# Local and global attention ahead of a feed-forward layer: block transposes on VectorE with an exchange through HBM, from the fifth pair of heads on

## The chip, the cores and the metric

The kernel runs on one core of a Trainium2 chip, as one launch. The metric is the device time of an execution in microseconds; several executions are timed and their median is compared. One more execution was taken with the hardware profiler, and all rows of a profile come from it. The engines are PE (TensorE matmul; PEld is its weight load), DVE (VectorE), ACT (ScalarE), POOL (GpSimd) and SP (SyncE, which issues all DMAs here).

## What is computed

A batch of 8 with 8 heads of 64: 512 local tokens attend to a window of 32 tokens to either side and to 32 global tokens; the 32 global tokens attend to everything. The attention output, 4608 rows of 512, goes through a feed-forward layer with a leaky activation whose slope is per feature. All is float32.

```python
s_ll = np.where(np.abs(pos[:, None] - pos[None, :]) <= 32, scale * q_l @ k_l.T, -1e9)
out_l = sm(concat([scale * q_l @ k_g.T, s_ll])) @ concat([v_g, v_l])
out_g = sm(scale * q_g @ concat([k_g, k_l]).T) @ concat([v_g, v_l])
x = concat([out_g, out_l]).transpose(0, 2, 1, 3).reshape(4608, 512)
h = x @ w_in
return (np.maximum(h, 0) + alpha * np.minimum(h, 0)) @ w_out
```

## The kernel before

**Pairs.** Two heads make a pair P (0 to 31; `NPAIR` = 4 pairs make a batch). Local attention of a pair has four parts. `local_scores` does 32 small matmuls (one for each of 16 windows of 32 queries and each head h, 64 rows deep, 128 keys wide) into two PSUM banks `s_ps`. `local_softmax` works on them: DVE scales, masks and takes a minimum (`p`, `mn`), ACT takes eight exponentials with sums. `local_transposes` lets PE transpose the probabilities `p` (eight 128x128 transposes into `pt`), and ACT and DVE copy one bank each to SBUF. `local_values` multiplies with the values `vw` into `o_ps`, and DVE scales by `rz` into `xq`. `local_outputs` lets PE transpose `xq` (four transposes, `xt`), and ACT copies them into `x_raw`, where the batch's four pairs lie side by side.

**Feed-forward.** 9 groups (8 batches of 512 local columns, then all 256 global columns) times 16 slices of the hidden width make 144 steps t. In step t `f1(t)` does 12 matmuls into a bank `h_ps`; ACT and DVE make `g` of it, ACT rounds `g` to `gh`, and POOL takes the rest `gl`. `f2` of the step two earlier does 8 matmuls with `gh` (part 0) and 4 with `gl` (part 1) into four output banks. These 24 matmuls are 512 columns wide, or 256 in the last group. Inputs and weights are split into a rounded part and a rest, hence three matmuls for each product. The 16 weight tiles `ws` arrive as words that DVE and ACT decode into `wt` during the first steps.

**Global attention.** 16 blocks k of two pairs: `global_scores` (`g_ps`), `global_transposes` (`gt`), `global_values` (`go`), `global_outputs` (again in the bank of `go`, into `x_glb`).

**Order.** Pairs 0 to 3 run ahead of step 0, with PE transposes and their own branch. All others are placed by hand: `plan(t, where, fn, P)` puts a part into step t ahead of f1 ("pre"), between f1 and f2 ("mid"), or between the two parts of f2 ("post"). Each pair has four steps: scores in "pre" of the first, transposes in "pre" of the third, values in its "post", outputs in "mid" of the fourth. A scheduler then sets the order on every engine; matmuls stay in program order. Each engine works its list in order, and SP issues its DMAs in order, waiting where a source or a buffer isn't ready.

**PSUM.** `h_ps` has two banks (tag "h"); s_ps, pt, o_ps, xt and all global parts of the later pairs share two others (tag "s"); four hold the outputs. `qk` and `vw` of the later pairs have one buffer each.

Of the kernel before, what the change touches and what calls it, by code (L numbers as in the profile page):

```python
# [8 lines left out]
F32 = mybir.dt.float32  # L9
# [8 lines left out]
NB, NH, SL, SG, D = 8, 8, 512, 32, 64  # L18
# [12 lines left out]
TC = dict(schedule_with_timeline_sim=True)  # L31
HP = 50
HPU = 4
PAD = (0, 0)
LAG = 2
NDEC = 2
NLOAD = 3
# [12 lines left out]
    return 32 * (3 * (i // 2) + i % 2)  # L50


@with_exitstack
def longformer_ffn(ctx: ExitStack, tc: tile.TileContext, qk, vs, gn, vg, w, alpha, out):
    nc = tc.nc
# [3 lines left out]
    work = ctx.enter_context(tc.tile_pool(name="work", bufs=1))  # L59
    psum = ctx.enter_context(tc.tile_pool(name="psum", bufs=1, space=PS))  # L60
    wpool = ctx.enter_context(tc.tile_pool(name="wpool", bufs=NWB))

    alpha_sb = const.tile([128, NF + PAD[0]], F32, name="alpha_sb")[:, 0:NF]
    mask = const.tile([128, 4, 128], F32, name="mask")
# [10 lines left out]
    def matmul(*a, **k):  # L75
        return tc.keep_in_program_order(nc.tensor.matmul(*a, **k))  # L76
# [4 lines left out]
    def stage(name, dtype=F32):  # L81
        return work.tile([128, 512], dtype, tag="st", name=name, bufs=NST)
# [10 lines left out]
    def bank(tag, name):  # L93
        return psum.tile([128, 512], F32, tag=tag, name=name, bufs=2 if tag in "hs" else 1)
# [29 lines left out]
    def wide(name, dtype=F32):  # L124
        return work.tile([128, 1024], dtype, tag="dec", name=name, bufs=3)
# [49 lines left out]
    def local_scores(P):  # L175
        t = qks.pop(P)
        tags = ("o0", "o1", "o2", "o3") if P < NPAIR else ("s", "s", "s", "s")
        for h in range(2):
            ps_of[P, h] = bank(tags[2 * (P % 2) + h], "s_ps")
            if P < NPAIR:  # L180
                matmul(ps_of[P, h], ident_bf, mask_bf, start=True, stop=False)
        for i in range(NWIN):
            for h in range(2):
                hs = slice(64 * h, 64 * h + 64)
                k0 = SL + window(i)
                r0, c0 = 32 * (i % 4), 128 * (i // 4)
                matmul(ps_of[P, h][r0 : r0 + 32, c0 : c0 + 128], t[hs, 32 * i : 32 * i + 32], t[hs, k0 : k0 + 128], start=P >= NPAIR, stop=P >= NPAIR or i >= NWIN - 4)

    def local_softmax(P):
        z = small("z", 8)  # L190
# [19 lines left out]
    def local_transposes(P):  # L210
        for h in range(2):
# [4 lines left out]
            pt_of[P, h] = stage("pt")  # L216
            copy("ad"[h], pt_of[P, h], ps)

    xs = {}

    def split(src, n):
        xh, xl = stage("xh", F32R), stage("xl", F32R)
        nc.scalar.copy(xh[:, 0:n], src)
        nc.vector.tensor_tensor(xl[:, 0:n], src, xh[:, 0:n].bitcast(F32), op=ALU.subtract)  # L224
        return xh, xl

    def local_values(P):
        o = bank("h" if P < NPAIR else "s", "o_ps")
        v = vws.pop(P)
        for i4 in range(4):  # L230
            for h in range(2):
                for k in range(4):
                    i = 4 * i4 + k
                    c = 128 * i4 + 64 * h
                    matmul(o[32 * k : 32 * k + 32, c : c + 64], pt_of[P, h][:, 32 * i : 32 * i + 32], v[:, i % 2, i // 2, 64 * h : 64 * h + 64], start=True, stop=True)
        z, rz = z_of.pop(P), small("rz", 8)
        nc.scalar.activation(rz, z, AF.Copy, bias=1e-9)
        nc.vector.reciprocal(rz, rz)
        xq = stage("xq")
        nc.vector.tensor_tensor(xq.rearrange("q (g d) -> q g d", g=8), o.rearrange("q (g d) -> q g d", g=8), sub_ap(rz, 0, 128, 0, ((1, 8), (0, 64))), op=ALU.mult)  # L240
        xq_of[P] = xq

    def local_outputs(P):
        b, p = divmod(P, NPAIR)
        xq = xq_of.pop(P)
        ps = bank("h" if P < NPAIR else "s", "xt")
        for i in range(4):
            transpose(ps[:, 128 * i : 128 * i + 128], xq[:, 128 * i : 128 * i + 128], ident)
        if P < NPAIR:
            xs[0, p] = split(ps, SL)  # L250
        else:
            nc.scalar.copy(x_raw[:, p], ps)  # L252

    gns, vgs, sgs, gz, gout = {}, {}, {}, {}, {}

    def load_global(k, what):
        for P in (2 * k, 2 * k + 1):
            if what == "gn":
                gns[P] = wide("gn")[:, 0:576]
                nc.sync.dma_start(gns[P], gn[P])  # L260
            else:
                vgs[P] = wide("vg")[:, 0:640].rearrange("k (y d) -> k y d", y=5)
                nc.sync.dma_start(vgs[P], vg[P])

    def global_scores(k):
        ss = [bank("s", "g_ps") for h in range(2)]
        for h in range(2):
            nc.vector.memset(ss[h][64:128, 256:288], -3.0e38)
        for r, c0, n in ((0, 32, 288), (1, 320, 256)):
            for e in range(2):  # L270
                t = gns[2 * k + e]
                for h in range(2):
                    hs, q0 = slice(64 * h, 64 * h + 64), 64 * r + 32 * e
                    matmul(ss[h][q0 : q0 + 32, 0:n], t[hs, 0:32], t[hs, c0 : c0 + n], start=True, stop=True)
        for e in range(2):
            del gns[2 * k + e]
        m, z = small("gm", 4), small("gz", 4)
        sg_sb = sgs[k] = wide("sg")[:, 0:576].rearrange("q (h n) -> q h n", h=2)
        for h in range(2):
            nc.vector.tensor_reduce(m[:, h : h + 1], ss[h][:, 0:288], axis=AX.X, op=ALU.max)  # L280
        nc.vector.tensor_scalar(m[:, 2:4], m[:, 0:2], -0.125, None, op0=ALU.mult)
        nc.vector.tensor_copy(m[0:64, 0:2], m[64:128, 2:4])
        nc.vector.tensor_tensor(m[0:64, 2:4], m[0:64, 2:4], m[0:64, 0:2], op=ALU.min)
        nc.vector.tensor_copy(m[64:128, 2:4], m[0:64, 2:4])
        for h in range(2):
            nc.scalar.activation(sg_sb[:, h], ss[h][:, 0:288], AF.Exp, bias=m[:, 2 + h : 3 + h], scale=0.125, accum_out=z[:, h : h + 1])
        nc.vector.tensor_copy(z[0:64, 2:4], z[64:128, 0:2])
        nc.vector.scalar_tensor_tensor(z[0:64, 2:4], z[0:64, 2:4], 1e-9, z[0:64, 0:2], op0=ALU.add, op1=ALU.add)
        nc.vector.reciprocal(z[0:64, 2:4], z[0:64, 2:4])
        nc.vector.tensor_copy(z[64:128, 2:4], z[0:64, 2:4])  # L290
        gz[k] = z
# [11 lines left out]
                nc.vector.transpose(sgt_sb[0:32, 4, h, 32 * e : 32 * e + 32], sg_sb[32 * e : 32 * e + 32, h, 256:288])  # L303

    def global_values(k):
        ps = bank("s", "go")
        for y in range(5):
            for h in range(2):
                for e in range(2):
                    q0 = 64 * h + 32 * e  # L310
                    matmul(ps[q0 : q0 + 32, 0:64], sgt_sb[:, y, h, 32 * e : 32 * e + 32], vgs[2 * k + e][:, y, 64 * h : 64 * h + 64], start=(y == 0), stop=(y == 4))
        for e in range(2):
            del vgs[2 * k + e]
        z = gz.pop(k)
        for h in range(2):
            hs = slice(64 * h, 64 * h + 64)
            nc.scalar.activation(og_sb[hs, hs], ps[hs, 0:64], AF.Copy, scale=z[hs, 2 + h : 3 + h])
        gout[k] = ps

    def global_outputs(k):  # L320
        ps = gout.pop(k)
        b, p = divmod(2 * k, NPAIR)
        matmul(ps[:, 64:128], og_sb, pick, start=True, stop=True)
        nc.scalar.copy(x_glb[:, p : p + 2, SG * b : SG * b + SG], ps[:, 64:128].rearrange("d (e q) -> d e q", e=2))
# [54 lines left out]
    def plan(t, where, fn, P):  # L379
        at.setdefault((t, where), []).append((fn, P))  # L380

    for P in range(NPAIR, NPR):
        base = 4 * (P - NPAIR)
        plan(base, "pre", local_scores, P)
        plan(base, "pre", local_softmax, P)
        plan(base + 2, "pre", local_transposes, P)
        plan(base + 2, "post", local_values, P)
        plan(base + 3, "mid", local_outputs, P)
        if P > NPAIR:
            plan(base - 4, "mid", load_qk, P)  # L390
            plan(base - 1, "post", load_v, P)
    begin = [16] + [20 + 8 * i for i in range(12)] + [112, 116, 120, 128]
    for k in range(NPR // 2):
        t = begin[k]
        late = begin[k + 1] - t < 8 or t == 120
        plan(t - 1, "mid", lambda k: load_global(k, "gn"), k)
        plan(t, "post", global_scores, k)
        plan(t + 1, "mid", lambda k: load_global(k, "vg"), k)
        when = ((2, "post"), (3, "mid"), (3, "post")) if late else ((3, "pre"), (6, "post"), (7, "mid"))
        for (dt, where), fn in zip(when, (global_transposes, global_values, global_outputs)):  # L400
            plan(t + dt, where, fn, k)

    def attention(t, where):
        for fn, P in at.pop((t, where), ()):
# [27 lines left out]
    load_next(NLOAD)  # L432
    load_qk(NPAIR)
    load_v(NPAIR)

    def scores(P):
        local_scores(P)
        local_softmax(P)

    keep_warm(6)  # L440
    scores(0)
# [94 lines left out]
```

## Time and profile before

| What | Value |
|---|---|
| median of 3 runs (lowest, highest) | 985.55 us (984.82, 986.91) |
| profiled execution, its time | 984.07 us |
| its span (first to last instruction) | 982.3 us |
| granted TensorE clock, mean | 0.981 |
| DMA packets and bytes | 88110, 102.55 MB |
| time of the packets, share of 16 engines | 31.0% |

A row of the timeline has the start, the length to the end of the last instruction in it, engine, line, operation, out<-in, shape and count. Matmuls overlap, so the pitch between starts and not the length tells what one costs. Small float32 matmuls show as two instructions each. A row of groups has the busy time, the mean length of one in ns, and the idle time of the engine ahead of it with what ended it. DMA rows end with KB and the median time from issue to landing.

### The profile page before, as it was taken

Reading aid. Unit: us, or ns where it says so; the run is one execution under the profiler, and the core shown is the slowest. Engines: PE = TensorE matmul, PEld = TensorE weight load, DVE = VectorE, ACT = ScalarE, POOL = GpSimd, SP = SyncE. Lnnn points to the kernel's source line nnn. Section 1 sums busy time; section 2 is a strip of 40 time slices with the busy share of each in tenths; the row PEclk is TensorE's granted clock in tenths of the full one; section 3 lists DMA queues with packets and bytes.
Section 4 is the critical chain, followed back from the end, with each engine's and each line's share of the span. In section 5 each row is a group of like instructions: output and inputs, shape, how many; then the busy total and the mean of one; then the engine's idle time right before and its main releaser. Section 6 shows DMA issues by size and latency. Waiting matters only on the chain.

```text
span 982.3 us, 21069 instructions
## 1 busy us (share of the span) xinstructions
PE 942.5 (96%) x8962; PEld 752.0 (77%) x8962; DVE 388.3 (40%) x765; ACT 421.2 (43%) x1139; POOL 183.3 (19%) x161
## 2 busy tenths in 40 slices
PE   5588899999999999999999999999999999999997
PEld 3466688778777887878787878878777777778797
DVE  4899952532342323332343224232343234222211
ACT  4776743543444334433453333443454333322232
POOL 1002221212111222122121112212212112222221
PEclk8788999999999999999999999999999999999999
DMA  9935432332324323322334223332233221210010
GB/s 317 379 144 206 139 96 72 116 106 84 111 85 135 102 67 100 127 67 73 110 103 135 84 84 108 102 110 69 73 126 111 84 83 27 93 51 28 0 44 22
DMA packets 88110, 102.55 MB, mean 104 GB/s; under 512 B 3536, under 2 KB 69584, under 8 KB 85968
## 3 DMA queue, kind: packets, MB, share of 16 engines
q1 hardware_dynamic: 88016, 101.21, 31.0%
q8 instruction: 70, 1.15, 0.5%
q14 instruction: 24, 0.20, 0.1%
HBM read 92.28 MB, written 8.91 MB: 103 GB/s over the span
## 4 chain that ended last, share of the span: by engine, by line
PE 87%; DVE 7%; SPq 2%; issue 1%; ACT 1%; DMA 1%; DVEq 0%; ACTq 0%
PE o L76 38%; PE h_ps L76 37%; PE o_ps L76 3%; PE s_ps L76 3%; PE pt L79 2%; SPq L171 1%; DVE wt L140 1%; PE go L76 1%; PE xt L79 1%; DVE wt L142 1%; DVE wt L137 1%; DVE wt L149 1%; PE g_ps L76 1%; DMA ws<-in_w_dram 1%; PE gt L79 1%
## 5 line engine op out<-in xcount | busy, mean ns | idle before, releaser
L76 PE MATMUL h_ps<-xh,wt 128*128 128x512 f32 (+1 forms) x1152 | 351.6, 388 | 0.0
L349 POOL TENSOR_TENSOR gl<-g,gh 128x512 fp32r<-128x512 f32 (+1 forms) x144 | 178.8, 1242 | 791.1 <-ACT gh L348 714.9
L76 PE MATMUL o<-gh,wt 128*128 128x512 f32 (+1 forms) x1152 | 279.7, 385 | 0.0
L76 PEld LDWEIGHTS h_ps<-xh,wt 128*128 128x128 f32 x1152 | 208.3, 189 | 45.6 <-issue 4.5
L76 PEld LDWEIGHTS o<-gh,wt 128*128 128x128 f32 x1152 | 206.6, 188 | 43.0
L346 DVE SCALAR_TENSOR_TENSOR g<-g,beta_sb,h_ps 128x512 f32<-128x512 f32 (+1 forms) x144 | 103.1, 716 | 319.4 <-ACT g L345 319.0
L76 PE MATMUL h_ps<-xl,wt 128*128 128x512 f32 (+1 forms) x576 | 220.6, 383 | 0.8 <-DVE xl L224 0.8
L345 ACT ACTIVATE g<-h_ps 128x512 f32<-128x512 f32 (+1 forms) x144 | 82.0, 569 | 223.6 <-PE h_ps L76 206.4
L76 PE MATMUL o<-gl,wt 128*128 128x512 f32 (+1 forms) x576 | 156.1, 393 | 0.0
L206 ACT ACTIVATE p<-p,mn 128x128 f32<-128x128 f32 x224 | 86.8, 390 | 107.4 <-DVE mn L203 107.4
L348 ACT CAST gh<-g 128x512 fp32r<-128x512 f32 (+1 forms) x144 | 85.9, 596 | 109.2 <-DVE g L346 109.1
L76 PEld LDWEIGHTS h_ps<-xl,wt 128*128 128x128 f32 x576 | 108.6, 189 | 24.0 <-DVE xl L224 1.2
L76 PEld LDWEIGHTS o<-gl,wt 128*128 128x128 f32 x576 | 101.5, 189 | 27.6 <-issue 7.2
L202 DVE SCALAR_TENSOR_TENSOR p<-s_ps,mask 128x512 f32<-128x512 f32 x56 | 36.0, 683 | 60.5 <-PE s_ps L76 60.5
L76 PEld LDWEIGHTS o_ps<-vw,pt 128*32 128x32 f32 x2048 | 31.5, 113 | 16.9 <-issue 10.4
L91 DVE COPY pt<-pt 128x512 f32<-128x512 f32 x32 | 22.1, 689 | 55.5 <-PE pt L79 55.5
L206 ACT ACTIVATION_READ_ACCUMULATOR p<-p,mn 128x1 f32 x224 | 42.0, 187 | 0.0
L76 PE MATMUL o_ps<-vw,pt 128*32 128x64 f32 x2048 | 37.1, 226 | 4.9 <-DVE pt L91 3.9
L79 PE MATMUL pt<-ident,p 128*128 128x128 f32 x256 | 37.2, 288 | 4.6 <-ACT p L206 4.5
L76 PEld LDWEIGHTS s_ps<-qk 64*32 64x32 f32 x2048 | 30.2, 110 | 13.6 <-issue 12.7
L79 PEld LDWEIGHTS pt<-ident,p 128*128 128x128 f32 x256 | 32.0, 147 | 10.7 <-issue 4.8
L76 PE MATMUL s_ps<-qk 64*32 64x128 f32 x2048 | 39.4, 285 | 0.7 <-ACT x_raw L252 0.7
(76 smaller groups left out, 565.5 us busy)
## 6 DMA issues: line engine op xcount, KB each, us to landing
vw<-in_vs_dram SPq DMA_DIRECT2D x64, 512.0 KB, 5.2
qk<-in_qk_dram SPq DMA_DIRECT2D x32, 672.0 KB, 4.0
ws<-in_w_dram SPq DMA_DIRECT2D x16, 1024.0 KB, 9.2
vg<-in_vg_dram SPq DMA_DIRECT2D x32, 320.0 KB, 3.1
gn<-in_gn_dram SPq DMA_DIRECT2D x32, 288.0 KB, 4.7
out_dram<-ost SPq DMA_DIRECT2D x32, 256.0 KB, 2.3
out_dram<-ost SPq DMA_DIRECT2D x4, 128.0 KB, 2.4
alpha_sb<-in_alpha_dram SPq DMA_DIRECT2D x1, 8.0 KB, 1.7
```

What stands on the lines that cost most here:

```text
L76: return tc.keep_in_program_order(nc.tensor.matmul(*a, **k))
L79: return tc.keep_in_program_order(nc.tensor.transpose(*a))
L91: nc.vector.tensor_copy(dst, src)
L137: nc.vector.tensor_scalar(t, t, CLAMP_LO, CLAMP_HI, op0=ALU.max, op1=ALU.min)
L140: nc.vector.scalar_tensor_tensor(tu, high, 0xC0000000, tu, op0=ALU.bitwise_and, op1=ALU.bitwise_or)
L142: nc.vector.tensor_tensor(ti, ti, r, op=ALU.add)
L202: nc.vector.scalar_tensor_tensor(p, s, -0.125, mask.rearrange("q i n -> q (i n)"), op0=ALU.mult, op1=ALU.add)
L206: nc.scalar.activation(p3[:, i], src[:, i], AF.Exp, bias=mn[:, i : i + 1], scale=scale, accum_out=z[:, k : k + 1])
L345: nc.scalar.activation(g[:, 0:n], h[:, 0:n], AF.Relu, scale=-1.0)
L346: nc.vector.scalar_tensor_tensor(g[:, 0:n], g[:, 0:n], beta_sb[:, f : f + 1], h[:, 0:n], op0=ALU.mult, op1=ALU.add)
L348: nc.scalar.copy(gh[:, 0:n], g[:, 0:n])
L349: nc.gpsimd.tensor_tensor(gl[:, 0:n], g[:, 0:n], gh[:, 0:n].bitcast(F32), op=ALU.subtract)
```

## The change

Four parts, all for pairs from the fifth on (P >= 4).

**Transposes.** `exchange` has DVE transpose the sixteen 32x32 blocks of a 128x512 tile in one instruction, with the blocks in another order, writes the tile to HBM in one DMA (128 rows of 2 KB), and reads it back in four (32 partitions each, 512 bytes a row), which puts the blocks on their partitions. It takes the place of the PE transposes and their copies, once for each head's probabilities (`pb`, into `pt`) and once for the output (`xb`, straight into `x_raw`). `place` numbers the windows so that blocks and windows agree.

**Order.** A pair's scores come in "post" of step turn[P], its values in "post" of turn[P+1], directly ahead of the next pair's scores. Turns are 0, 3, 7, 10, 13, then every four steps from 17.

**Global parts.** o_ps and go move from the "s" banks to the two "h" banks. The 16 blocks are spread evenly over steps 17 to 124; values of one block stand directly ahead of scores of the next; outputs get a place and a bank (`gx`) of their own. `gn` and `sg` live in one weight slot.

**Addresses.** `PAD` makes two tiles larger, which moves what is allocated behind them. Of the staging tiles (the moving operands of f1 and f2) the address in a partition was 256 bytes past a multiple of 512 and is a multiple of 512; of the weight tiles it was 128 past one and is a multiple.

```diff
-PAD = (0, 0)
+PAD = (64, 32)
+def place(P, c, wd):
+    return 4 * c + wd if P < NPAIR else 4 * wd + c
...
+    def exchange(src, put, name):
+        blk = stage(name)
+        nc.vector.transpose(blk.rearrange("k (b c n) -> k c b n", b=4, c=4), src.rearrange("q (c b n) -> q c b n", c=4, b=4))
+        spread = dram.tile([128, 4, 128], F32, tag=name, name=name, bufs=2)
+        nc.sync.dma_start(spread, blk.rearrange("k (b n) -> k b n", b=4))
+        for b in range(4):
+            nc.sync.dma_start(put[32 * b : 32 * b + 32].rearrange("k (w n) -> k w n", w=4), spread[:, b].rearrange("(w k) n -> k w n", w=4))
+
+    def local_exchange(P):
+        for h in range(2):
+            pt_of[P, h] = stage("pt")
+            exchange(pr_of.pop((P, h)), pt_of[P, h], "pb")
...
     def local_values(P):
-        o = bank("h" if P < NPAIR else "s", "o_ps")
+        o = bank("h", "o_ps")
...
-        xq_of[P] = xq
+        if P < NPAIR:
+            xq_of[P] = xq
+        else:
+            exchange(xq, x_raw[:, P % NPAIR], "xb")
...
     def global_values(k):
-        ps = bank("s", "go")
+        ps = bank("h", "go")
...
     def global_outputs(k):
-        ps = gout.pop(k)
+        ps = bank("s", "gx")
...
+    turn = {4: 0, 5: 3, 6: 7, 7: 10, 8: 13}
     for P in range(NPAIR, NPR):
-        base = 4 * (P - NPAIR)
-        plan(base, "pre", local_scores, P)
-        plan(base, "pre", local_softmax, P)
-        plan(base + 2, "pre", local_transposes, P)
-        plan(base + 2, "post", local_values, P)
-        plan(base + 3, "mid", local_outputs, P)
+        u = turn.setdefault(P + 1, 4 * (P - NPAIR) + 1)
+        plan(u, "post", values, P)
+        if P == NPAIR:
+            plan(turn[P], "post", scores, P)
+        if P + 1 < NPR:
+            plan(u, "post", scores, P + 1)
+            plan(turn[P] + 1, "post", load_qk, P + 1)
+            plan(u + 1, "post", load_v, P + 1)
...
+        plan(u, "mid", global_scores, k)
+        plan(v - 2, "mid", global_transposes, k)
+        at.setdefault((v, "mid"), []).insert(0, (global_values, k))
+        plan(v + 1, "mid", global_outputs, k)
```

On PE, in the middle of the program, between the two parts of an f2 (`o_` and a number are the four output banks; x32 counts matmuls), before:

```order
L76 MATMUL o_4318<-gh,wt 128x512 x2
L76 MATMUL o_ps<-vw,pt 32x64 x32
L76 MATMUL go<-vg,sgt_sb 32x64 x20
L76 MATMUL o_4315<-gl,wt 128x512
L76 MATMUL o_4316<-gl,wt 128x512
```

On PE at the same place, now:

```order
L81 MATMUL o_4552<-gh,wt 128x512 x2
L81 MATMUL o_ps<-vw,pt 32x64 x32
L81 MATMUL s_ps<-qk 32x128 x32
L81 MATMUL o_4549<-gl,wt 128x512
L81 MATMUL o_4550<-gl,wt 128x512
```

The scores of the next pair stand behind the values, and the global values have gone elsewhere.

On DVE during the decoding of the weights (`wt` is a weight tile being decoded, ISA one of its operations), before, up to the eighth `g`:

```order
L346 SCALAR_TENSOR_TENSOR g<-g,beta_sb,h_ps 128x512
L142 ISA wt<-wt,wr 128x2048
L137 TENSOR_SCALAR wt<-wt 128x1024
L240 TENSOR_TENSOR xq<-o_ps,rz 128x512
L139 TENSOR_SCALAR wt<-wt 128x1024
L149 TENSOR_TENSOR wt<-wt 128x2x512
L140 SCALAR_TENSOR_TENSOR wt<-ws,wt 128x1024
L346 SCALAR_TENSOR_TENSOR g<-g,beta_sb,h_ps 128x512
```

On DVE with as many weights decoded, now, up to the fifth `g`:

```order
L145 SCALAR_TENSOR_TENSOR wt<-ws,wt 128x1024
L228 STREAM_TRANSPOSE pb<-p 128x4x4x32
L147 ISA wt<-wt,wr 128x2048
L142 TENSOR_SCALAR wt<-wt 128x1024
L144 TENSOR_SCALAR wt<-wt 128x1024
L154 TENSOR_TENSOR wt<-wt 128x2x512
L145 SCALAR_TENSOR_TENSOR wt<-ws,wt 128x1024
L368 SCALAR_TENSOR_TENSOR g<-g,beta_sb,h_ps 128x512
```

The transpose of pair 5 stands where values of pair 5 stood, and three fewer steps have been through.

On SP in the steady part, before (loads of the next pairs and global blocks):

```order
L171 DMA vw<-in_vs_dram 128x8x128 x2
L260 DMA gn<-in_gn_dram 128x576
L160 DMA qk<-in_qk_dram 128x1344
L263 DMA vg<-in_vg_dram 128x640 x2
L171 DMA vw<-in_vs_dram 128x8x128 x2
```

On SP in the steady part, now:

```order
L176 DMA vw<-in_vs_dram 128x8x128 x2
L230 DMA xb<-xb 128x512
L165 DMA qk<-in_qk_dram 128x1344
L232 DMA x_raw<-xb 32x4x128 x4
L230 DMA pb<-pb 128x512
L286 DMA vg<-in_vg_dram 128x640 x2
L281 DMA gn<-in_gn_dram 128x576
L232 DMA pt<-pb 32x4x128 x4
L230 DMA pb<-pb 128x512
L281 DMA gn<-in_gn_dram 128x576
L232 DMA pt<-pb 32x4x128 x4
```

The 15 transfers of an exchange stand among the loads, each write ahead of the four reads that wait for its landing.

More of the change, by code (lines that the diff above doesn't have):

```diff
@@ L61, in longformer_ffn @@
     wpool = ctx.enter_context(tc.tile_pool(name="wpool", bufs=NWB))
+    dram = ctx.enter_context(tc.tile_pool(name="dram", bufs=1, space=bass.MemoryType.DRAM))
     alpha_sb = const.tile([128, NF + PAD[0]], F32, name="alpha_sb")[:, 0:NF]
@@ L181, in local_scores @@
                 matmul(ps_of[P, h], ident_bf, mask_bf, start=True, stop=False)
-        for i in range(NWIN):
+        for j in range(NWIN):
+            c, wd = divmod(j, 4)
+            i = place(P, c, wd)
             for h in range(2):
@@ L185, in local_scores @@
                 k0 = SL + window(i)
-                r0, c0 = 32 * (i % 4), 128 * (i // 4)
-                matmul(ps_of[P, h][r0 : r0 + 32, c0 : c0 + 128], t[hs, 32 * i : 32 * i + 32], t[hs, k0 : k0 + 128], start=P >= NPAIR, stop=P >= NPAIR or i >= NWIN - 4)
+                r0, c0 = 32 * wd, 128 * c
+                matmul(ps_of[P, h][r0 : r0 + 32, c0 : c0 + 128], t[hs, 32 * i : 32 * i + 32], t[hs, k0 : k0 + 128], start=P >= NPAIR, stop=P >= NPAIR or c == 3)
     def local_softmax(P):
@@ L232, in local_values @@
                 for k in range(4):
-                    i = 4 * i4 + k
+                    i = place(P, i4, k)
                     c = 128 * i4 + 64 * h
@@ L240, in local_values, with load_gn, load_vg @@
         nc.vector.tensor_tensor(xq.rearrange("q (g d) -> q g d", g=8), o.rearrange("q (g d) -> q g d", g=8), sub_ap(rz, 0, 128, 0, ((1, 8), (0, 64))), op=ALU.mult)
-        xq_of[P] = xq
+        if P < NPAIR:
+            xq_of[P] = xq
+        else:
+            exchange(xq, x_raw[:, P % NPAIR], "xb")
     def local_outputs(P):
-        b, p = divmod(P, NPAIR)
         xq = xq_of.pop(P)
-        ps = bank("h" if P < NPAIR else "s", "xt")
+        ps = bank("h", "xt")
         for i in range(4):
             transpose(ps[:, 128 * i : 128 * i + 128], xq[:, 128 * i : 128 * i + 128], ident)
[L249 to L256, printed above, removed]
-        for P in (2 * k, 2 * k + 1):
[L258 to L263, printed above, removed]
+        xs[0, P] = split(ps, SL)
+    gns, vgs, sgs, gz = {}, {}, {}, {}
+    big = []
+    def load_gn(k):
+        if not big:
+            big.append(wpool.tile([128, 2048], F32, tag="w", name="gn"))
+        for e in range(2):
+            gns[2 * k + e] = big[0][:, 576 * e : 576 * e + 576]
+            nc.sync.dma_start(gns[2 * k + e], gn[2 * k + e])
+    def load_vg(k):
+        for P in (2 * k, 2 * k + 1):
+            vgs[P] = wide("vg")[:, 0:640].rearrange("k (y d) -> k y d", y=5)
+            nc.sync.dma_start(vgs[P], vg[P])
     def global_scores(k):
@@ L277, in global_scores @@
         m, z = small("gm", 4), small("gz", 4)
-        sg_sb = sgs[k] = wide("sg")[:, 0:576].rearrange("q (h n) -> q h n", h=2)
+        sg_sb = sgs[k] = big[0][:, 1152:1728].rearrange("q (h n) -> q h n", h=2)
         for h in range(2):
@@ L317, in global_values @@
             nc.scalar.activation(og_sb[hs, hs], ps[hs, 0:64], AF.Copy, scale=z[hs, 2 + h : 3 + h])
-        gout[k] = ps
     def global_outputs(k):
-        ps = gout.pop(k)
+        ps = bank("s", "gx")
         b, p = divmod(2 * k, NPAIR)
@@ L380, in plan, with scores, values @@
         at.setdefault((t, where), []).append((fn, P))
-    for P in range(NPAIR, NPR):
-        base = 4 * (P - NPAIR)
-        plan(base, "pre", local_scores, P)
-        plan(base, "pre", local_softmax, P)
-        plan(base + 2, "pre", local_transposes, P)
-        plan(base + 2, "post", local_values, P)
-        plan(base + 3, "mid", local_outputs, P)
[L389 to L392, printed above, removed]
-    for k in range(NPR // 2):
[L394 to L401, printed above, removed]
+    def scores(P):
+        local_scores(P)
+        local_softmax(P)
+        if P >= NPAIR:
+            local_exchange(P)
+    def values(P):
+        local_values(P)
+    turn = {4: 0, 5: 3, 6: 7, 7: 10, 8: 13}
+    for P in range(NPAIR, NPR):
+        u = turn.setdefault(P + 1, 4 * (P - NPAIR) + 1)
[6 more added lines that the diff above has]
+            plan(u + 1, "post", load_v, P + 1)
+    step = []
+    for j in range(NPR // 2 + 1):
+        u = 17 + 107 * j // 16
+        step.append(u + (u % 4 == 1))
+    for k in range(NPR // 2):
+        u, v = step[k], step[k + 1]
+        plan(u - 2, "mid", load_gn, k)
+        plan(u, "mid", global_scores, k)
+        plan(u + 1, "mid", load_vg, k)
+        plan(v - 2, "mid", global_transposes, k)
+        at.setdefault((v, "mid"), []).insert(0, (global_values, k))
+        plan(v + 1, "mid", global_outputs, k)
     def attention(t, where):
@@ L434, in longformer_ffn @@
     load_v(NPAIR)
-    def scores(P):
-        local_scores(P)
-        local_softmax(P)
     keep_warm(6)
```

## The prediction

> **What bounds the kernel now.** I read the page first, then busy time by stage, then the chain of waits where the stages meet.
>
> ```profile
> span 982.3 us, 21069 instructions
> PE 942.5 (96%) x8962; PEld 752.0 (77%) x8962; DVE 388.3 (40%) x765; ACT 421.2 (43%) x1139; POOL 183.3 (19%) x161
> PE 87%; DVE 7%; SPq 2%; issue 1%; ACT 1%; DMA 1%; DVEq 0%; ACTq 0%
> ```
>
> ```profile
> 64.00:122.46 58.46, 50.89 (x449) 39.69 (x449) 57.57 (x64) 41.70 (x78) 11.54 (x8) 0.93 0.57 204
> 122.46:925.00 802.54, 802.54 (x7450) 636.95 (x7450) 274.30 (x610) 323.93 (x925) 154.84 (x121) 1.00 0.28 89
> ```
>
> ```profile
> 117.92 0.66 PE xt L79 x4
> 118.58 2.79 PE o L76 x12
> 121.37 1.09 PE s_ps L76 x64
> 122.46 2.98 PE h_ps L76 x12
> ```
>
> The columns of the stage rows are stretch, length, PE, PEld, DVE, ACT, POOL, clock, DMA share, GB/s. Up to 122.46 DVE is the bound (57.57 of 58.46 us): it decodes the weights. From 122.46, where f1(8) starts behind the scores of pair 6, PE is never idle (802.54 of 802.54). So work taken from PE after that is worth its full price, and before that nothing.
>
> **The change part by part.** The timeline of PE (start, length) prices its blocks:
>
> ```profile
> 301.78 1.10 PE L76 MATMUL o_ps<-vw,pt 128*32 128x64 f32 x64
> 302.70 0.74 PE L76 MATMUL go<-vg,sgt_sb 128*32 128x64 f32 x40
> ...
> 307.19 0.60 PE L79 MATMUL xt<-ident,xq 128*128 128x128 f32 x4
> 307.63 0.33 PE L76 MATMUL go<-pick,og_sb 128*128 128x64 f32 x2
> 307.77 2.11 PE L76 MATMUL o<-gh,wt 128*128 128x512 f32 x8
> 309.72 1.08 PE L76 MATMUL o<-gl,wt 128*128 128x512 f32 x4
> 310.73 1.16 PE L76 MATMUL s_ps<-qk 64*32 64x128 f32 x64
> 311.81 0.73 PE L76 MATMUL h_ps<-xh,wt 128*128 128x512 f32 x2
> ...
> 312.61 0.64 PE L76 MATMUL h_ps<-xh,wt 128*128 128x512 f32 x2
> ...
> 321.11 2.03 PE L76 MATMUL o<-gh,wt 128*128 128x512 f32 x8
> 322.97 1.09 PE L76 MATMUL o<-gl,wt 128*128 128x512 f32 x4
> 323.90 1.03 PE L79 MATMUL pt<-ident,p 128*128 128x128 f32 x8
> ...
> 325.47 0.63 PE L76 MATMUL h_ps<-xh,wt 128*128 128x512 f32 x2
> ...
> 327.56 2.03 PE L76 MATMUL o<-gh,wt 128*128 128x512 f32 x8
> 329.53 1.10 PE L76 MATMUL o_ps<-vw,pt 128*32 128x64 f32 x64
> 330.56 1.20 PE L76 MATMUL o<-gl,wt 128*128 128x512 f32 x4
> 331.60 0.60 PE L79 MATMUL gt<-ident,sg 128*128 128x128 f32 x4
> ```
>
> A big matmul takes (322.97 - 321.11) / 8 = 0.2325 us, a step of 24 of them 5.58.
>
> *Transposes off PE.* pt: 325.47 - 323.90 less three matmuls (0.70) = 0.87. xt: 307.63 - 307.19 = 0.44. Pairs 6 to 31 have both after 122.46: 26 x 1.31 = 34.1 us less.
>
> *Values beside scores.* Values alone cost 331.60 - 327.56 less twelve matmuls (2.79) = 1.25: eight matmuls ahead of them take 1.97 instead of 1.86, four behind them 1.04 instead of 0.93, so 0.11 each for going in and out. Followed by other small matmuls the block takes 0.92 (302.70 - 301.78) instead of 1.03. Scores: 312.61 - 309.72 less seven matmuls (1.62) = 1.27. Side by side, one way out and one way in go: 0.2 a pair, 25 pairs: 5 us less (bounds 0 and 5.5).
>
> *Global blocks.* go leaves the values and joins g_ps, which changes nothing; gx loses its neighbour xt and pays its own way in: about 0.11 x 16 = 2 us more.
>
> *The decode stage.* DVE gets three block transposes a pair for one copy, and scores of pair 4 start behind f1(0) instead of ahead of it. The bank of f1(6) is that of f1(4), so f1(6) starts when the fifth g is done. From where the two orders of DVE part, the new one has, up to the end of the fifth g, the same decode work and softmaxes as the old one up to the eighth, but five transposes for two copies, one xq and three g.
>
> ```profile
> 117.19 0.68 DVE L240 TENSOR_TENSOR xq<-o_ps,rz 128x512 f32<-128x512 f32 x1
> 117.79 0.68 DVE L139 TENSOR_SCALAR wt<-wt 128x1024 uint32<-128x1024 uint32 x1
> 120.66 0.74 DVE L346 SCALAR_TENSOR_TENSOR g<-g,beta_sb,h_ps 128x512 f32<-128x512 f32 x1
> 121.31 1.21 DVE L142 CUSTOM_DVE_ANT_0 wt<-wt,wr 128x2048 uint16<-128x2048 uint16 x1
> ```
>
> ```profile
> L303 DVE STREAM_TRANSPOSE sgt_sb<-sg 32x32 f32<-32x32 f32 x64 | 12.8, 200 | 12.3 <-ACT sg L286 11.3
> ```
>
> One 128x512 operation holds DVE 0.60 us (117.79 - 117.19), a g 0.65. No row has a 128x512 transpose; its bounds are 16 blocks in one stream at an operation's 0.60 and 16 separate ones at 0.2 = 3.2; I take 0.65, since it is one instruction of 512 elements a partition. Five of them are 3.3, what they replace 3 x 0.60 + 3 x 0.65 = 3.8: a wash. So f1(6) starts near 121, where the eighth g ended before (at 3.2 each it would be 134). Two steps (11.2) and one block of values and scores (1.25 + 1.27 - 0.2) then bring f1(8) to 134.5 instead of 122.46: 12.0 us more.
>
> *The exchange.* It costs PE nothing while it is covered by the four steps between scores(P) and values(P). SP issues 15 more transfers a pair, and waits on a landing ahead of each four reads; behind it stand qk, vw, gn and vg, none needed within two steps. ACT loses two copies a pair.
>
> ```profile
> out_dram<-ost SPq DMA_DIRECT2D x32, 256.0 KB, 2.3
> vw<-in_vs_dram SPq DMA_DIRECT2D x64, 512.0 KB, 5.2
> ```
>
> ```profile
> 330.69 1.01 SPq L171 DMA_DIRECT2D vw<-in_vs_dram  x2
> ...
> 316.64 0.39 ACT L206 ACTIVATE p<-p,mn 128x128 f32<-128x128 f32 x1
> ```
>
> After the scores (last matmul before 311.81) the exponentials end at 317.03, 5.2 us on; the first half's transpose can end at about 4.5. Then in series: first write, four reads issued (0.5 each), second write, four issues, last read: 4.5 + 4 + 3 landings. At 2.3 us each, as 256 KB go to HBM in the out rows, 15.4; values come 4 x 5.58 = 22.3 after the scores (16.7 in two early turns of three steps). Covered: 0. The Trainium skill's page "VectorE: DVE Perf Modes" (Rules for kernel authors) gives 128x128 transposes to TensorE and leaves VectorE only 32x32 blocks. By that rule the 39 us on PE would stay and the time with them, 985.5. The row 122.46:925.00 (PE full, DVE 274.30 of 802.54) speaks against it; the row ahead of it bears it out.
>
> *Addresses.* Moving tiles go from 256 past a multiple of 512 to a multiple, weights from 128 past one.
>
> ```profile
> 31.57 1.05 PE L76 MATMUL warm<-idle 128*128 128x512 f32 x2
> 32.42 0.41 PE L79 MATMUL pt<-ident,p 128*128 128x128 f32 x1
> ...
> 952.85 1.12 PE L76 MATMUL o<-gh,wt 128*128 128x256 f32 x8
> 953.80 0.64 PE L76 MATMUL o<-gl,wt 128*128 128x256 f32 x4
> ```
>
> ```profile
> 28.00:34.00 6.00, 3.77 (x15) 3.28 (x16) 5.14 (x10) 5.21 (x20) 0.00 (x0) 0.50 1.03 370
> ```
>
> At clock 0.50 a 512-column matmul takes 0.425 us; half of that is 213 ns, so at full clock there are 19 ns in excess, and at 256 columns 119 - 107 = 12. Extended to no columns, 119 - (232.5 - 119) = 5.5 ns are fixed, the rest grows with width, as a start address would not. No row has another address; the bounds for the start address are 0 and 5.5, and I take the middle, 2.7 ns, on 122 x 24 + 384 = 3312 matmuls after 121: 9 us less. The whole excess is a rival.
>
> **Sum.** 982.3 - 34.1 - 5 + 2 + 12 - 9 = 948.2 as span. The profiled execution took 984.07, 1.8 over its span, and the median is 1.5 over that: 951.5 us.
>
> **The rivals.**
> *A2, addresses do nothing:* 960.5. It is the same case with another size.
> *B, the addresses take the whole excess,* because both read streams pay for crossing: 2928 x 19 + 384 x 12 = 60 us off 960.5: 900. For it: the excess is there in every row of full clock; against: none at half clock, at the same addresses. The Trainium skill's "TensorE: Matmul & The Clock Gate" (section "Wait — 56ns, not 53.3ns?") has warm matmuls N / 2.4 GHz + 2.5 ns apart, 216 ns at 512 columns; the trace's 232.5 disagrees, and by that formula the time would be about 909.
> *C, the exchange is late, slower than before:* PE waits at values for pt. The vw rows, of 512 bytes as the reads here, land in 5.2. Three such landings make 24.1, that is 1.8 late in 23 pairs and 7.4 in two: 56 us, 1008. It starts to bite at 4.6 us a landing and turns gain to loss at 4.9. Against it: DMA share is 0.28.
> *D, values in the h banks:* o_ps and go take one of f1's two banks, so the next f1 but one may wait for a g that stands behind exponentials on ACT and transposes on DVE. At 1 us for each of 25 pairs, 977.
>
> **How the numbers follow.** A with A2 0.52 (own range 940 to 964), B or most of it 0.20, D and lesser stalls 0.18, C 0.10. The range 910 to 970 leaves out the full B, most of C and the worse half of D. A difference of 0.2% is about what a measurement here can tell from none. Faster: A, B, nearly all of D, 0.02 of C: 0.89; same 0.02; slower 0.09.
>
> **What would show it.** PE without pt and xt blocks behind 122; o_ps and s_ps adjacent without a gap; a pitch of big matmuls of 232.5 (A2), 230 (A) or 214 ns (B); f1(6) near 121, held by a g; no idle of PE ahead of o_ps released by a DMA (else C) and none ahead of h_ps released by DVE (else D). Wrong it would be by a transpose much over 0.65 us, or by a DMA that lands later than 4.6.

## The result, and the profile after

| | before | after |
|---|---|---|
| median | 985.55 us (5 runs, 984.65 to 986.91) | 994.42 us (5 runs, 991.02 to 996.21) |
| profiled execution, span | 982.3 us | 993.8 us |
| f1(8) starts at | 122.39 us | 137.35 us |
| from there to the start of the last f1 | 848.97 us | 845.83 us |

The ratio is 1.0084, with an interval of 1.0058 to 1.011: slower by 0.8%, where 951.5 us was predicted. Two questions follow. f1(8) starts 15.0 us later (12 were predicted; the table has the start of its first matmul, the stage rows of before begin at 122.46). The rest is only 3.1 us shorter (46 were predicted). The page after: span, engines, the granted clock by slices, and the chain.

```profile
span 993.8 us, 21228 instructions
PE 909.2 (91%) x8624; PEld 730.6 (74%) x8626; DVE 428.5 (43%) x821; ACT 391.4 (39%) x1083; POOL 184.9 (19%) x161
PEclk8667799989999999989999999989999999999999
PE 73%; DMA 8%; DVE 7%; SPq 5%; ACT 5%; issue 2%; DVEq 0%; ACTq 0%
```

PE works 33 us less than before (942.5). That is less than the 46 us that were to go, and about 12 us of the difference are matmuls at a lower clock, as shown below. Its share of the chain fell from 87% to 73%, and after the start the clock has slices below full speed again. The stage behind f1(8) (same columns as the stage rows of before):

```profile
137.35:925.00 787.65, 755.13 (x7088) 603.69 (x7087) 305.91 (x652) 289.57 (x862) 150.86 (x118) 0.98 0.44 143
```

Behind 137.35 PE, which was never idle there before, is idle for 787.65 - 755.13 = 32.5 us, and its mean clock is 0.98 instead of 1.00. The largest waits of PE in that part (waiter, what released it, us in all, times, longest):

```profile
PE o L81 <- ACT ost L94: 20.6, 6, 4.6
PE h_ps L81 <- DVE xl L244: 5.0, 7, 0.8
PE h_ps L81 <- DVE g L368: 4.8, 1, 4.8
PE o_ps L81 <- DMA pt<-pb: 1.7, 2, 0.9
```

The largest is not among the prediction's rivals. It stands where a batch's first f2 (step 16m+2) needs the four output banks, which `ost` copies must have emptied. The timeline of PE and ACT at the first such place:

```profile
197.14 1.97 PE L81 MATMUL o<-gh,wt 128*128 128x512 f32 x8
199.04 1.10 PE L81 MATMUL o_ps<-vw,pt 128*32 128x64 f32 x64
200.07 1.16 PE L81 MATMUL s_ps<-qk 64*32 64x128 f32 x64
201.16 1.20 PE L81 MATMUL o<-gl,wt 128*128 128x512 f32 x4
202.19 0.62 PE L81 MATMUL h_ps<-xh,wt 128*128 128x512 f32 x2
...
205.01 0.69 PE L81 MATMUL g_ps<-gn 64*32 64x288 f32 x16
210.30 3.78 PE L81 MATMUL o<-gh,wt 128*128 128x512 f32 x8 [4.60 <-ACT ost L94]
213.88 1.71 PE L81 MATMUL o<-gl,wt 128*128 128x512 f32 x4
```

```profile
203.59 0.40 ACT L213 ACTIVATE p<-p,mn 128x128 f32<-128x128 f32 x1 [4.16 <-DVE g_ps L291]
...
208.70 0.50 ACT L309 ACTIVATE gn<-g_ps,gm 128x288 f32<-128x288 f32 x1 [1.68 <-DVE gm L307]
...
209.66 2.05 ACT L94 COPY ost<-o 128x512 f32<-128x512 f32 x4
```

The last matmul of the old batch starts before 202.19, so the banks are full from then on. But ScalarE's list has the eight exponentials of the pair first, then those of a global block, which wait for VectorE; the copies begin at 209.66. Before, a pair's scores stood ahead of f1(16m), and its exponentials were over by then. ScalarE at the same batch, before (the last of the eight exponentials, then the copies):

```profile
181.33 0.39 ACT L206 ACTIVATE p<-p,mn 128x128 f32<-128x128 f32 x1
...
187.87 2.04 ACT L89 COPY ost<-o 128x512 f32<-128x512 f32 x4
```

Where no global block starts in step 16m+2, the wait is 2.3 to 2.4 us; with one it is 4.4 to 4.6.

The wait costs more than its length: the eight matmuls behind it take 213.88 - 210.30 = 3.58 us instead of 1.81 (e7's row below, with the same weight address). By the pitch of their starts, matmuls at the lower clock behind five of the six waits and behind the one below cost about 12 us more than at full clock; behind the sixth (at 642.80) the clock stayed full.

The wait of 4.85 us is seen along three engines:

```profile
649.04 0.38 SPq L230 DMA_DIRECT2D pb<-pb  x1
653.40 0.78 SPq L232 DMA_DIRECT2D pt<-pb  x2
654.23 1.89 SPq L397 DMA_DIRECT2D out_dram<-ost  x4
```

```profile
656.43 0.60 ACT L367 ACTIVATE g<-h_ps 128x512 f32<-128x512 f32 x1 [7.14 <-DMA out_dram<-ost]
```

```profile
657.86 1.22 PE L81 MATMUL h_ps<-xh,wt 128*128 128x512 f32 x2 [4.85 <-DVE g L368]
```

SP waits at the reads for the write's landing (649.04 to 653.40), the four `out_dram` transfers stand behind it, and a `g` waits, by the profile, for one of them: the transfer still holds a staging tile. ScalarE names this release five times in that part, 30.5 us in all; once it reached PE.

### The profile page after: what moved, and what is told of

The parts are those of the page before. It is cut to its first block, busy times and chain, and to the rows that moved or that the text cites. A ratio compares the mean times of both kernels' runs of the same rounds, so it can differ in the third digit from the quotient of the medians.

```text
span 993.8 us, 21228 instructions
## 1 busy us (share of the span) xinstructions
PE 909.2 (91%) x8624; PEld 730.6 (74%) x8626; DVE 428.5 (43%) x821; ACT 391.4 (39%) x1083; POOL 184.9 (19%) x161
## 4 chain that ended last, share of the span: by engine, by line
PE 73%; DMA 8%; DVE 7%; SPq 5%; ACT 5%; issue 2%; DVEq 0%; ACTq 0%
PE o L81 33%; PE h_ps L81 32%; PE o_ps L81 3%; PE s_ps L81 3%; DMA ws<-in_w_dram 2%; ACT p L213 2%; DMA pb<-pb 2%; SPq L232 2%; DMA xb<-xb 2%; SPq L176 2%; DVE xl L244 1%; DVE p L209 1%; SPq L134 1%; DVE wt L145 1%; PE go L81 1%
## 5 line engine op out<-in xcount | busy, mean ns | idle before, releaser
L81 PE MATMUL h_ps<-xh,wt 128*128 128x512 f32 (+1 forms) x1152 | 346.5, 384 | 30.5 <-DVE g L368 29.6
L81 PE MATMUL o<-gh,wt 128*128 128x512 f32 (+1 forms) x1152 | 284.6, 390 | 20.6 <-ACT ost L94 20.6
L81 PEld LDWEIGHTS h_ps<-xh,wt 128*128 128x128 f32 x1152 | 215.6, 192 | 75.5 <-DVE g L368 31.3
L81 PEld LDWEIGHTS o<-gh,wt 128*128 128x128 f32 x1152 | 209.0, 193 | 68.4 <-ACT ost L94 24.4
L81 PE MATMUL o<-gl,wt 128*128 128x512 f32 (+1 forms) x576 | 153.1, 388 | 0.0
L81 PEld LDWEIGHTS o<-gl,wt 128*128 128x128 f32 x576 | 104.5, 191 | 24.9 <-issue 5.4
L228 DVE STREAM_TRANSPOSE pb<-p 128x512 f32<-128x512 f32 x56 | 39.8, 712 | 30.6 <-ACT p L213 30.2
L81 PEld LDWEIGHTS o_ps<-vw,pt 128*32 128x32 f32 x2048 | 32.5, 116 | 13.6 <-DVE g L368 7.8
L260 DVE TENSOR_TENSOR xq<-o_ps,rz 128x512 f32<-128x512 f32 x32 | 22.1, 691 | 44.6 <-PE o_ps L81 44.6
L210 DVE TENSOR_REDUCE mn<-p 128x4 f32<-128x512 f32 x56 | 35.4, 660 | 0.0
```

Source lines behind the costliest of these rows:

```text
L210: nc.vector.tensor_reduce(mn, p3, axis=AX.X, op=ALU.min)
L228: nc.vector.transpose(blk.rearrange("k (b c n) -> k c b n", b=4, c=4), src.rearrange("q (c b n) -> q c b n", c=4, b=4))
```

## The experiments

All times below are medians, and each ratio is to the kernel before on the same chip (985.5 to 986.1 us).

**e1: values and scores behind f2's second part, at six steps.**

```diff
+        here = (u + 1, "pre") if u % NF == 1 else (u, "post")
-        plan(u, "post", values, P)
+        plan(*here, values, P)
...
-            plan(u, "post", scores, P + 1)
+            plan(*here, scores, P + 1)
```

> At the six steps 16m+1 that carry values and scores of a pair, both stand behind the four matmuls of f2's second part instead of ahead of them; nothing else is edited, and ScalarE's list now has the four ost copies ahead of the exponentials. Theory 1 (TensorE waits for the four output banks, because the copies that empty them stand on ScalarE behind exponentials and the global block's chain): the six waits (4.60 + 2.44 + 4.40 + 2.32 + 2.43 + 4.39 = 20.6 us) go, and the matmuls at half clock behind them (about 11 us), so 994.4 - 32 = 962 us, 957 if the wait of 4.85 us at 657.86 goes with them. Rival (the copies are late for want of a staging tile that a transfer to HBM still holds, or because f2's matmuls end late): the waits stay, 994 us.

Measured: 954.19 us, ratio 0.9675 (0.9652 to 0.9697). Four matmuls changed places with a block in six steps, and 40 us went. ScalarE at the first of these places, and the stage row:

```profile
194.98 2.05 ACT L94 COPY ost<-o 128x512 f32<-128x512 f32 x4
200.11 0.40 ACT L213 ACTIVATE p<-p,mn 128x128 f32<-128x128 f32 x1 [3.08 <-DVE g_ps L291]
```

```profile
137.35:925.00 787.65, 778.60 (x7345) 630.07 (x7344) 309.66 (x660) 298.94 (x875) 161.16 (x129) 1.00 0.44 142
```

The copies come first, no o waits for ost, the idle time is 9.05 us instead of 32.5, the clock is 1.00, and the wait for a staging tile went too. 20.6 + 4.85 + 12 make 37 of the 40 us. In the profiled executions f1(8) starts 5.8 us earlier here (131.55), though every engine has the same order up to there, so this is spread; the two together are the 43.4 us by which the spans differ (993.8 and 950.4). Theory 1 stands and its rival falls.

**e2, e3, e6, e7: the addresses.** `PAD` alone: e2 is the kernel before with (64, 32), e3 the changed kernel with (0, 0); e6 is before with (64, 0), e7 before with (0, 96).

> The kernel before with the two paddings alone. Theory (the start address of the tiles costs 5.6 ns a big matmul): 3312 matmuls x 5.6 ns = 18.5 us less, 967 us, a plain step 5.44 us instead of 5.58. The prediction's middle (2.7 ns): 976.5. Rival (the shorter pitch comes from the new order or from the transposes that are gone, not from addresses): 985.5 us, 5.58.

> The changed kernel without the two paddings. Theory (addresses, 5.6 ns a big matmul): a plain step is 5.58 again and the time 994.4 + 18 = 1012 us. Rival (addresses do nothing): 994 us.

> The kernel before with the staging tiles (moving operands) at multiples of 512 bytes, and the weight tiles at 384 past one. If the moving operand's start sets the pitch, all of the 13.5 us of both paddings: 972.5 us. If the weights' start does: 986 us. Half of it: 979 us.

> The kernel before with the weight tiles at multiples of 512 bytes, and the staging tiles still at 256 past one. If the moving operand's start sets the pitch: 986 us. If the weights' start does: 972.5 us.

| kernel | moving tiles past a multiple of 512 | weights | us | ratio (interval) |
|---|---|---|---|---|
| before | 256 | 128 | 985.7 to 986.1 | |
| e2 | 0 | 0 | 972.57 | 0.9865 (0.9844 to 0.9887) |
| e6 | 0 | 384 | 985.5 | 1.0003 (0.9994 to 1.0013) |
| e7 | 256 | 0 | 972.86 | 0.9873 (0.9856 to 0.9889) |
| e3 (after) | 256 | 128 | 1007.5 | 1.0215 (1.0193 to 1.0237) |

e3 is 13.1 us above the changed kernel, e2 13.5 below the one before. e7 has 12.8 of the 13.5 (the intervals overlap) and e6 nothing: it comes from the start address of the weights, not from that of the moving operand. The second padding moves whatever is allocated behind it, not the weight tiles alone, but the rows below are of matmuls that read nothing but `gh` or `gl` and `wt`. A plain f2 of e6 and one of e7:

```profile
322.18 2.03 PE L76 MATMUL o<-gh,wt 128*128 128x512 f32 x8
324.05 1.09 PE L76 MATMUL o<-gl,wt 128*128 128x512 f32 x4
```

```profile
317.88 1.98 PE L76 MATMUL o<-gh,wt 128*128 128x512 f32 x8
319.69 1.07 PE L76 MATMUL o<-gl,wt 128*128 128x512 f32 x4
```

1.87 / 8 = 0.234 us against 1.81 / 8 = 0.226. The 13.5 us on 3312 matmuls are 4.1 ns each, not the 5.6 of the expectation. A plain step does fall from 5.58 to 5.44 us, as expected, but steps with small matmuls gain less, and the 256-column ones nothing (by their starts in the last group 118.7 ns before, 120.0 in e7).

**e4: the old front.** Pairs 4 to 7 with TensorE transposes and the places and banks of before.

```diff
+    for P in range(NPAIR, EX):      # EX = 8
+        base = 4 * (P - NPAIR)
+        plan(base, "pre", scores, P)
+        plan(base + 2, "pre", local_transposes, P)
+        plan(base + 2, "post", values, P)
+        plan(base + 3, "mid", local_outputs, P)
...
-        if P >= NPAIR:
+        if P >= EX:
             local_exchange(P)
```

> Pairs 4 to 7 keep the PE transposes and the places of the kernel before; from pair 8 on everything is as in the changed kernel. Theory 1: f1(8) is back near 122.5 instead of 137.4 (14.9 us less), pairs 6 and 7 have their PE transposes again (2 x 1.31 = 2.6 more), and the waits behind stay: 994.4 - 14.9 + 2.6 = 982 us. Rival (VectorE's load while it decodes sets the start, whatever stands in the order, since the global blocks and later exchanges only move forward): 990 us or more.

Measured: 980.05 us, ratio 0.9938 (0.9919 to 0.9957), 14.4 below the changed kernel, with f1(8) at 121.22. The front's loss is undone by the front alone; the six waits for `ost` are still there, 20.6 us.

**e5: TensorE transposes in e1's order.** As in e1, with `local_transposes` two steps behind the scores and `local_outputs` behind the values, for all pairs.

> The order and the addresses of the run with the copies first (954.2 us), but all pairs go through TensorE transposes with their PSUM banks and copies, as in the kernel before; the exchange is gone. Theory (what the exchange takes from TensorE is worth its full price once nothing else is waited for): 26 pairs x 1.31 = 34 us more on TensorE, less up to 6 us where VectorE is unburdened while it decodes: 982 to 988 us. Rival (most of the 40 us of that run came from elsewhere, and the transposes are partly hidden): under 970 us.

Measured: 1000.36 us, ratio 1.0157 (1.0136 to 1.0179): 46 us more than e1, beyond both expectations. Its waits for the "s" banks behind f1(8) say part of why:

```profile
PE g_ps L81 <- DVE g_ps L292: 8.3, 8, 1.3
PE pt L84 <- ACT gn L310: 3.8, 3, 1.7
PE pt L84 <- ACT x_raw L272: 1.5, 1, 1.5
```

The transposes bring back their own time and these 13.6 us of waits besides, and the front gained little (f1(8) at 128.58, 131.55 in e1): 34.1 + 13.6 - 3.0 = 44.7 us. The profiled executions differ by 51.4 us, so some 7 us of theirs stay unexplained. The exchange takes two kinds of load away: matmul time and PSUM banks. In this order it is worth more than the 34 us of the sum.

**e8: values and scores ahead of f1 of every fourth step, on top of e4.**

```diff
-        u = turn.setdefault(P + 1, 4 * (P - NPAIR) + 1)
+        u = turn.setdefault(P + 1, 4 * (P - NPAIR) + (P == EX))
-        plan(u, "post", values, P)
+        plan(u, "pre", values, P)
...
-            plan(u, "post", scores, P + 1)
+            plan(u, "pre", scores, P + 1)
...
-        step.append(u + (u % 4 == 1))
+        step.append(u + (u % 4 == 1 or u % 4 == 0))
```

> The changed kernel with pairs 4 to 7 as in the kernel before, and from pair 9 on values and scores in front of f1 of every fourth step (step 17, then 20, 24, 28, ...), so that exponentials are done before the output banks have to be emptied and the first f1 of a batch has other work ahead of it; global scores keep away from these steps. Theory: 954.2 of the run with the copies first, less 14.4 (old front, 994.4 - 980.0), less about 5 for the waits of h_ps for xl: 935 us. Rival (one more step of delay at the exchange or the staging tiles shows next): 945 us or more, with waits of o_ps for a DMA.

Measured: 952.89 us, ratio 0.9667 (0.9641 to 0.9694), so the rival's number. None of PE's waits names a DMA; the three longest:

```profile
PE o L81 <- ACT ost L94: 5.9, 2, 4.0
PE s_ps L81 <- ACT gn L310: 2.7, 2, 2.0
PE h_ps L81 <- DVE xl L244: 2.1, 3, 0.9
```

The pairs' exponentials are out of the way of the copies, and what remains is the global block's chain: at step 18 it stands ahead of the copies alone and costs 3.96 us. Behind the other wait for `ost` (1.91 us), though, the copies themselves wait, by the profile for a staging tile that a write of `pb` still holds, so the rival's second half is there as well:

```profile
612.04 2.05 ACT L94 COPY ost<-o 128x512 f32<-128x512 f32 x4 [2.30 <-DMA pb<-pb]
```

The waits for xl fell from seven to three, all at places where no block stands ahead of the batch's first f1.

**e9: e1 and e4 together.**

> The changed kernel with two edits together: pairs 4 to 7 as in the kernel before, and the block of values and scores behind f2's second part at the steps 16m+1. Theory (both repairs are independent): 994.4 - 40.2 - 14.4 = 940 us, f1(8) near 121, no wait of o for ost. Rival (one eats the other, since both fill the same time): about 953, as in the run before.

Measured: 942.26 us, ratio 0.9565 (0.9549 to 0.9581): 52 of the 54.6 us add up.

```profile
PE h_ps L81 <- DVE xl L244: 4.8, 7, 0.8
PE h_ps L81 <- ACT xh L243: 1.0, 2, 0.5
```

Nothing else is waited for behind f1(8).

**e10: e9 with the split of three x tiles ahead of a batch's last f1.**

> The same, and the split of the next batch's first three x tiles stands ahead of the last f1 of a batch instead of behind it. If the waits of h_ps for xl at the starts of the batches (about 0.7 to 1.2 us each, 5 us together) come from the split standing behind ScalarE's and VectorE's work on g: 935 us. If x itself lands late from the exchange, nothing changes: 940 us, or more where g now waits behind the split.

Measured: 944.38 us, ratio 0.9582 (0.9568 to 0.9597): no gain. The wait moves to the fourth tile, whose split now stands behind the delayed `g` and `gh`. Both expectations missed half of it: the order of the split matters, and moving three of four doesn't mend it. Besides, two waits close together (0.95 us at 280.50, 0.65 at 281.88) were followed here by half clock, which e9 has nowhere behind f1(8) up to its last matmuls; it cost about 1.8 us.

**e11: e8 with the global blocks at other steps.**

```diff
+    step = [22, 30, 37, 42, 46, 54, 62, 69, 74, 78, 86, 94, 101, 106, 110, 118, 124]
```

> The run e8 (old front; values and scores in front of f1 of every fourth step) with one thing more: the 16 global blocks start at steps 22, 30, 37, 42, 46, 54, 62, 69, 74, 78, 86, 94, 101, 106, 110, 118, so none stands in the three steps around a batch's start or one step ahead of a pair's scores. Theory (what was left in e8 is the global block's chain on ScalarE ahead of the copies and ahead of the scores' banks, 10 us of waits, and half clock behind the long ones): 952.9 - 12 = 940 us, and the waits for xl at the batches' starts stay away, as in e8, so about 938. Rival (e8's loss against e9 lies in the early pairs, at every fourth step's spacing): 950 us.

Measured: 939.61 us, ratio 0.953 (0.9505 to 0.9554), 46 us below the kernel before and the fastest run.

```profile
PE o L81 <- ACT ost L94: 2.7, 2, 1.5
PE h_ps L81 <- DVE xl L244: 1.9, 3, 0.8
```

Moving only global blocks took 13 us off e8: the wait of 3.96 us behind a global block's chain is gone, which shows the same mechanism a second time, without the pairs. In the traces PE's waits behind f1(8) fell from 12.5 us to 4.6, and with the half clock behind that one wait (1.7 us) this is about 10 of the 13 us. What is left of `ost` is of the other kind, copies that wait for a staging tile held by a write of `pb`:

```profile
700.39 2.05 ACT L94 COPY ost<-o 128x512 f32<-128x512 f32 x4 [3.27 <-DMA pb<-pb]
```

Whether e11 beats e9 is not settled by these runs (939.6 with 937.5 to 941.2, against 942.3 with 942.0 to 943.2, each beside its own runs of before).

## Why the prediction was wrong

| term of the sum | predicted | measured |
|---|---|---|
| transposes off PE | -34.1 | not measured alone; e5: 46 with the banks |
| values beside scores | -5 | -4.5 |
| front | +12.0 | +15.0 in the trace, +9.2 in e1's with the same order; e4: -14.4 when undone, two pairs' PE transposes included |
| addresses | -9 | -13.5 (e2), -13.1 (e3) |
| exchange | 0 | 1.7 us for pt, at the two early turns of three steps |
| split of x at the batches' starts | not in it | about +5 (5.0 for xl, 0.9 for xh, against 0.8 before) |
| output banks, staging tile, lower clock | not in it | +37 (e1: -40) |

**The step that failed** is "So work taken from PE after that is worth its full price", as "Values beside scores" used it for the new order. The move was priced by PE's own matmuls alone (5 us less), and what it does to the other engines' lists was put at nothing. The full price holds only while PE goes on waiting for nothing; in its place the runs showed 32.5 us of idle time of PE behind 137.35, where there was none, and e1 took 40 us off by moving the block alone, with the exchange as it was.

I followed each moved part to what waits for its own result (pt, xq, x) and to the PSUM banks it takes, but not to the work that shares ScalarE's list with it. A move of the scores from ahead of f1(16m) to behind f2's first part of step 16m+1 moves eight exponentials to exactly the place where four copies must free the output banks, and a global block's chain stands there too in three batches of six. What is queued behind was asked for SP and for g, and not for `ost`. Rival D named ScalarE's and VectorE's lists, but as f1's bank waiting for g; its price of 977 had the wrong victim.

"It costs PE nothing", of the exchange, held but for two things. Of what stands behind its reads on SP the prediction named qk, vw, gn and vg and left out `out_dram`, whose late transfers hold staging tiles: the wait of 4.85 us. And at the two early turns of three steps PE waited 1.7 us for pt: at the first of them pt came 17.6 us behind the scores (136.32 to 153.98), where 15.4 were reckoned.

**What each wait drags behind it** was missing too. Matmuls behind a wait can run at half clock for some microseconds; I read that state in the rows of the start of the program, and used it only for the address. Two waits of nearly the same length, in the kernel after:

```profile
535.20 3.12 PE L81 MATMUL o<-gh,wt 128*128 128x512 f32 x8 [2.32 <-ACT ost L94]
538.11 1.72 PE L81 MATMUL o<-gl,wt 128*128 128x512 f32 x4
```

```profile
642.80 2.22 PE L81 MATMUL o<-gh,wt 128*128 128x512 f32 x8 [2.43 <-ACT ost L94]
644.86 1.09 PE L81 MATMUL o<-gl,wt 128*128 128x512 f32 x4
```

Eight matmuls take 2.91 us behind the wait of 2.32 and 2.06 behind that of 2.43, against 1.81. In the granted clock of this trace, half clock comes in stretches of 3.41 or 6.83 us; behind f1(8) they begin at 208.38, 317.61, 426.84, 536.06, 655.53 and 757.93, each 30, 32 or 35 times 3.413 us behind the one before it. The Trainium skill's page "TensorE: Matmul & The Clock Gate" (Part 1: The HAM clock gate) puts the drop at an idle window of about 3.4 us. The trace has that length, but PE need not be idle for all of it: the clock fell at 536.06 behind 2.32 us of idle. On the same grid that wait lies within one stretch of 3.41 us, and the wait at 642.80 is split over two (1.51 and 0.92 us), which would explain the difference; no run varied it.

**The front** was right in its place: f1(6) held by the fifth g.

```profile
121.08 0.74 DVE L368 SCALAR_TENSOR_TENSOR g<-g,beta_sb,h_ps 128x512 f32<-128x512 f32 x1
```

```profile
121.88 1.22 PE L81 MATMUL h_ps<-xh,wt 128*128 128x512 f32 x2 [13.45 <-DVE g L368]
```

The prediction had 121. Of the 3 us that it is short, 2 are the matmuls of f1(6), which ran at half clock behind 13.45 us of idle: f1(6) to f1(8) took 15.5 us where 13.5 were reckoned. That 134.5 came within 3 us is partly luck: e1, with the same order up to there, had f1(8) at 131.55.

**Addresses:** the size lay between my middle and my upper bound, and rival B (900) is out. The prediction placed the cause on the start address of moving tiles and weights alike; it is that of the weights alone. Its argument for the size, a fixed part that 256-column matmuls share, fails: these gained nothing.

**The exchange and the DVE transpose** were well sized:

```profile
L228 DVE STREAM_TRANSPOSE pb<-p 128x512 f32<-128x512 f32 x56 | 39.8, 712 | 30.6 <-ACT p L213 30.2
```

```profile
pb<-pb SPq DMA_DIRECT2D x56, 256.0 KB, 2.1
pt<-pb SPq DMA_DIRECT2D x224, 64.0 KB, 2.0
xb<-xb SPq DMA_DIRECT2D x28, 256.0 KB, 5.5
```

0.71 us a transpose (of sixteen 32x32 blocks in each group of 32 partitions, 64 in all) where 0.65 was taken, landings of 2.1 and 2.0 where 2.3 was taken and 4.6 would have bitten at turns of four steps, so rival C is out (xb lands later, issued right behind the loads of vw, and is needed later). The Trainium skill's page "VectorE: DVE Perf Modes" (Rules for kernel authors) gives 128x128 transposes to TensorE, as the prediction weighed. e5 speaks against it here: TensorE is the bound, and going back to it costs 46 us.

**Values beside scores:** the block takes 202.19 - 197.14 - 2.71 = 2.34 us beside twelve plain matmuls (0.226 each), instead of 1.25 + 1.27 = 2.52.

The predicted difference of the spans was -34.1 us. With the front as traced (+3), the addresses (-4.5), the waits for xl, xh and pt (+6.8) and those for output banks and a staging tile with the lower clock (+37) it would have been about +8; the spans differ by 11.5.

## What to carry to other kernels

When a block of work moves, follow it on every engine it uses, and ask on each list what now stands behind it: the cheap copies that free a buffer at a boundary between tiles are the ones that the bounding engine waits for. Price a wait of the bounding matmul engine with the lower clock that can follow it. Put blocks with long chains of exponentials a step or two away from such boundaries, and keep some independent matmuls ahead of the first one that needs a fresh split.

## What was not expected of the hardware

- The start of a weight tile in a partition sets the pitch of 512-column matmuls: 0.226 us at a multiple of 512 bytes (e7), 0.2325 at 128 past one (before) and 0.234 at 384 past one (e6). Other offsets were not tried. The start of the moving tile (0 or 256 past) does nothing (e2 and e7: 972.57 and 972.86 us). 256-column matmuls did not gain.
- Half clock can follow a wait of TensorE of 2.32 us (535.20, after) and even two of 0.95 and 0.65 us within 2 us (280.50, e10), but it need not: 2.43 us (642.80, after) and the same two waits later in e10 (592.11) left the clock full. After single waits of 0.7 us at the batches' starts the clock stayed full too.
